# Row maxima of an attention kernel: how they are transposed, copied into q's tile, and shared out between two stages

## The chip, the core and the metric

The kernel runs on one core of a Trainium2 chip. The metric is the device time of one execution in microseconds. The core has five engines that run on their own instruction streams and meet at semaphores: TensorE (PE in the profile; its weight loads are PEld), VectorE (DVE), ScalarE (ACT), GpSimd (POOL) and SyncE (SP), which here does nothing but issue DMA transfers.

## The reference, cut to what matters

Four layers over a sequence of 2048 rows of 512 numbers, all in float32: a Fourier mixing layer (A), attention (B), A again and B again, each behind a layer norm and with a residual sum.

```python
def _A_ref(x, dft_seq_re, dft_seq_im, dft_hid_re, dft_hid_im):
    a = jnp.einsum("bsd,ed->bse", x, dft_hid_re)
    b = jnp.einsum("bsd,ed->bse", x, dft_hid_im)
    return jnp.einsum("ts,bse->bte", dft_seq_re, a) - jnp.einsum("ts,bse->bte", dft_seq_im, b)

def _B_ref(x, wq, wk, wv, wo):          # 32 heads of 16, one head of keys and values for all
    ...
    scores = jnp.einsum("bhqd,bkd->bhqk", q, k) * (Dh ** -0.5)
    p = _softmax(scores, axis=-1)
    o = jnp.einsum("bhqk,bkd->bhqd", p, v)
    return (lambda x, *d: x.transpose(*d))(o, 0, 2, 1, 3).reshape(B, S, H * Dh) @ wo

x = A_x
x = x + _A_ref(_layernorm(x, axis=-1), ...)
x = x + _B_ref(_layernorm(x, axis=-1), ...)
x = x + _A_ref(_layernorm(x, axis=-1), ...)
x = x + _B_ref(_layernorm(x, axis=-1), ...)
```

## The kernel before, in words

The program handles one Fourier layer and the attention layer behind it as a pair (`make_layer`), twice. `phase_a` is the Fourier stage and `phase_b` the attention stage. The order on each engine is the order in which the Python program writes the instructions; nothing is reordered afterwards, so a step's place in the loops sets its place in the queue of its engine.

**Precision.** Most products are made of three matmuls (`mm3`, L87 to L89) of a rounded high part and a low remainder. ScalarE makes the high part, GpSimd or VectorE the low one (`split_sb`, `split_act`, `split_ps`).

**Fourier stage.** 128 steps: four column blocks (`tb`) of 512, two parts (`c`, real and imaginary), sixteen row tiles (`s`). A step has four products of three matmuls. After each of the first three blocks come four `y_tile` calls, which multiply by the hidden Fourier matrix, add the residual and take layer norm's statistics. The block's rows are then normalized (`ln_apply`, L182), transposed, and multiplied to keys, values and queries while the next block's steps run (`prep_tasks`). Queries are stored to DRAM (`qd`) and loaded again by tile (`qT_load`, L356).

**Early maxima.** Softmax needs each row's maximum ahead of the exponentials. A unit of maxima is one tile of 128 queries against one block of 512 keys: 32 matmuls with a VectorE maximum each (`max_one`, L334 and L335). The list `EARLY` names the units that are done in the Fourier stage already: tile, key block, the buffer for q, the step at which q is loaded, and the first and last place between which the 32 pieces are spread. Places count 40 to a block: 32 steps, and 8 for the four `y_tile` calls, one place being twelve matmuls. Before, the list has 16 units. The others are done in the attention stage (`max_half`, L347 and L348). A maximum uses one of three PSUM banks named `y`.

**Attention stage.** 16 tiles of 32 steps. Each step has four score matmuls (`score`, L698, two to one exponential of ScalarE, L701), three maxima for a later tile, and the eight matmuls of p times v of the step before last (`pv`, L712). Score and maximum matmuls use half the rows of the array, and the order alternates the halves.

**The maxima's rows.** The negated maxima of a tile are made part of the score product: q's tile has two spare rows in each half (rows 48, 49 and 112, 113) that hold the maximum's high and low part, against ones in the key tile. At step 27 `max_neg` reduces the next tile's partial maxima to `ms`; at step 29 `max_rows` transposes `ms` on TensorE into a `y` bank, ScalarE copies the result to `mt`, and four DMAs from SyncE's queue copy 16 of its rows each into one spare row of q's tile (L376 to L383). The first score of the next tile is at step 0, three steps later. The same is done for the second half of tile 0 and of tile 15, at steps 11 and 13, for step 16, and once at the end of the Fourier stage, where two of the four DMAs go on ScalarE's queue.

**Output projection.** At step 12 `o_proj` makes twelve matmuls for the tile before; after every six of them it also does two maxima, and adds them to the allowance (`owed`) of maxima per step. VectorE then adds the residual (L777).

Of the kernel before, what the change touches and what calls it, by code (L numbers as in the profile page):

```python
# [8 lines left out]
F32 = mybir.dt.float32  # L9
F32R = mybir.dt.float32r  # L10
I32 = mybir.dt.int32
AF = mybir.ActivationFunctionType
ALU = mybir.AluOpType
# [4 lines left out]
P = 128  # L18
# [4 lines left out]
NT = S // P  # L23
# [9 lines left out]


EARLY = [
# [5 lines left out]
]  # L41
KEPT = [e for e in EARLY if e[0]]
QSLOT = (8, 0, 1, "h", "l", 8, 0, 1, "h", "l", 8, 0, 1, 8, 0, 1)
# [4 lines left out]
def fnet_mqa_kernel(ctx: ExitStack, tc: tile.TileContext, x_in, ct, dt_, wq, wkv, wo, out):  # L48
    nc = tc.nc
    ctx.enter_context(tc.manual_schedule())  # L50
    sb = ctx.enter_context(tc.tile_pool(name="sb", bufs=1, reuse_waits="tile"))
# [3 lines left out]
    def f(ap):  # L55
        return ap.bitcast(F32)

    def slot(k, dtype=F32):
        return sb.tile([P, S], dtype, name=f"slot{k}")

    def half(k, dtype=F32):
        return sb.tile([P, D], dtype, name=f"row{k}")

    def bank(tag):
        return ps.tile([P, 512], F32, name=tag, bufs={"y": 3, "z": 1}[tag])
# [25 lines left out]
    ident = sb.tile([P, P], F32, name="ident")  # L91
# [18 lines left out]
    mv = sb.tile([P, NT, 2], F32, name="mv")  # L110
    rs = sb.tile([P, NT], F32, name="rs")
# [41 lines left out]
    def ln_rstd(t0, n, table=True, between=lambda: None):  # L153
        v = sb.tile([P, 4], F32, name="lnv", bufs=2)[:, :n]
        w = sb.tile([P, 4], F32, name="lnw", bufs=2)[:, :n]
        r = rs[:, t0:t0 + n]
        nc.vector.tensor_scalar(v, mv[:, t0:t0 + n, 1], EPS, None, op0=ALU.add)
        if table:
            nc.scalar.activation(w, v, AF.Sqrt)
            between()  # L160
            nc.vector.reciprocal(r, w)
            between()
            rounds = 1
        else:
            nc.vector.tensor_scalar(w.bitcast(I32), v.bitcast(I32), 1, None, op0=ALU.logical_shift_right)
            nc.vector.tensor_scalar(r.bitcast(I32), w.bitcast(I32), -1, 0x5F3759DF, op0=ALU.mult, op1=ALU.add)
            rounds = 3
        e = nc.vector if table else nc.gpsimd
        for _ in range(rounds):
            if n == 1 and table:  # L170
                e.scalar_tensor_tensor(w, r, v, r, op0=ALU.mult, op1=ALU.mult)
            else:
                e.tensor_mul(w, r, r)
                e.tensor_mul(w, w, v)
            between()
            e.tensor_scalar(w, w, -0.5, 1.5, op0=ALU.mult, op1=ALU.add)
            between()
            e.tensor_mul(r, r, w)
            between()

    def ln_apply(dst, x, t, eng=None):
        (eng or nc.vector).tensor_scalar(dst, x, mv[:, t, 0:1], rs[:, t:t + 1], op0=ALU.subtract, op1=ALU.mult)  # L182

    class Layer:
        pass
# [1 line left out]
    def make_layer(L, src, mid, dst, last):  # L187
        o = Layer()
        raws = {}
        hls = {}  # L190
        st = {}
# [41 lines left out]
        def wq_load(g):  # L233
            st["wq", g] = half(g)
            nc.sync.dma_start(st["wq", g], wq[:, g, :])

        def wq_split(g):
            st["wqh", g] = hl_tiles()
            split_sb(st["wq", g], *st["wqh", g], nc.gpsimd)
# [6 lines left out]
        def tr_tile(t, x, xth, xtl, raw=None):  # L246
            pt = bank("z")
            for k in range(NK):
                nc.tensor.transpose(pt[:, k * P:(k + 1) * P], x[:, k * P:(k + 1) * P], ident)
            v = [ap.rearrange("p (a b) -> p a b", a=NK) for ap in (pt, raw or pt)]  # L250
            if raw:
                split_act(v[0], xth, xtl, v[1])
            else:
                split_ps(v[0], xth, xtl)

        def kv(t0, n, xth, xtl, vt=None):
            pk = bank("y")[:, :n * P]
            for k in range(NK):
                mm3(pk, wkvh[:, k, :], wkvl[:, k, :], xth[:, k, :n * P], xtl[:, k, :n * P], k == 0, k == NK - 1)
            cs = slice(t0 * P, (t0 + n) * P)  # L260
            if vt is None:
                vt = half(7)[:64, :n * P]
            nc.scalar.copy(vt[32:64], pk[32:64])
            for g in range(2):
                gs = slice(64 * g, 64 * g + 64)
                nc.scalar.activation(kz[g][gs, cs], pk[gs], AF.Identity, scale=kmask[gs], bias=kone[gs])
            for g in range(2):
                gs = slice(64 * g + 32, 64 * g + 48)
                nc.vector.tensor_sub(kz[g][gs, cs], pk[gs], f(kz[g][gs, cs]))
            return vt  # L270

        def v_tr(t0, n, vt):
            pv_ = bank("z")[:, :n * 32].rearrange("p (t d) -> p t d", t=n)
            for j in range(n):
                nc.tensor.transpose(pv_[:, j, :], vt[32:64, j * P:(j + 1) * P], ident[32:64, 32:64])
            nc.scalar.copy(v1[:, t0:t0 + n, :DH], pv_[:, :, DH:])
# [95 lines left out]

        def max_rows(i, p0=0, n=NPAIR, queue=None):
            queue = queue or nc.sync
            pt = bank("y")[:4 * n, :P]
            nc.tensor.transpose(pt, st["ms"].rearrange("p a b c -> p (a b c)"), ident)  # L376
            mt = sb.tile([64, P], F32R, name="mt")[:4 * n, :]
            nc.scalar.copy(mt, pt)  # L378
            for g in range(2):
                for r in range(2):  # L380
                    row = 64 * g + M0 + r
                    q = queue if r else nc.sync
                    q.dma_start(f(o.qT[i][row:row + 1, p0:p0 + n, :]), f(mt[n * (2 * g + r):n * (2 * g + r + 1), :]))  # L383

        def y_tile(tb, tt, zh, zl, x1, between={}):
            t = 4 * tb + tt
# [82 lines left out]
        def prep_tasks(tb, x1):  # L469
            base = 32 * (tb + 1)  # L470
            ts = {}

            def alloc():
                ln_rstd(4 * tb, 4)
                st["xt"] = [slot(2 + j, F32R).rearrange("p (k t) -> p k t", k=NK) for j in range(2)]

            def tr(tt):
                xth, xtl = st["xt"]
                cs = slice(tt * P, (tt + 1) * P)
                tr_tile(4 * tb + tt, x1[tt], xth[:, :, cs], xtl[:, :, cs], half(6 + tt % 2))  # L480

            def do_kv():
                st["vt"] = kv(4 * tb, 4, *st["xt"])

            ts[0] = [alloc, lambda: ln_apply(x1[0], x1[0], 4 * tb, nc.gpsimd)]
            for j in range(1, 4):
                ts[j] = [lambda j=j: ln_apply(x1[j], x1[j], 4 * tb + j, nc.gpsimd), lambda j=j: tr(j - 1)]
            ts[4] = [lambda: tr(3)]
            ts[4] += [lambda: [wq_load(g) for g in range(4)]]
            ts[5] = [do_kv]  # L490
            ts[6] = [lambda: wq_split(0), lambda: v_tr(4 * tb, 4, st["vt"])]
            for g in range(4):
                ts[7 + g] = [lambda g=g: q_mm(tb, g, *st["xt"])]
                if g:
                    ts[7 + g].append(lambda g=g: q_store(tb, g - 1))
                if g < 3:
                    ts[7 + g].append(lambda g=g: wq_split(g + 1))
            ts[11] = [lambda: q_store(tb, 3)]
            return {base + k: v for k, v in ts.items()}

        def phase_a(extra):
# [155 lines left out]
            for k in range(12):  # L657
                more_max()
                if k == 2:
# [3 lines left out]
        units = [(0, pr, g, 3) for pr in range(HALF, NPAIR) for g in range(2)]  # L663
        units += [(i, pr, g, kb) for i in range(1, NT) for pr in range(NPAIR) for kb in range(4) for g in range(2)
                  if (i, kb) not in early]
        o.done = o.extra = 0

        def more_max():
            if o.done < len(units) and units[o.done][0] in o.loaded | {0}:
                max_half(*units[o.done])  # L670
                o.done += 1

        def owed(n):
            return min(3 * (n + 1) + 12 + o.extra, len(units)) - o.done

        def done_with(i, pr):
            return all(u[:2] > (i, pr) for u in units[o.done:])
# [83 lines left out]
        def o_mm(k):  # L761
            if k == 0:
                bt["po"] = bank("y")
            ks = slice(k * P, (k + 1) * P)
            mm3(bt["po"], bt["oh"][:, ks], bt["ol"][:, ks], woh[:, k, :], wol[:, k, :], k == 0, k == NK - 1)

        def o_proj(i):
            for k in range(NK):
                o_mm(k)
                if k % 2 and i < NT - 1:  # L770
                    for _ in range(2):
                        more_max()
                        o.extra += 1
            o_add(i)

        def o_add(i):
# [170 lines left out]
```

## Time and profile before

| | |
|---|---|
| median of 3 runs | 3785.59 us (3784.23 to 3785.99) |
| the profiled execution | 3786.89 us |
| its span, first to last instruction | 3784.9 us |
| mean granted TensorE clock | 0.993 |
| first Fourier stage and start | 0 to 711 us |
| first attention stage | 711 to about 1890 us |
| second Fourier stage | to about 2592 us |
| second attention stage | to the end |
| busy: PE, DVE, ACT, POOL | 97%, 74%, 63%, 20% |

In the rows of the profile a line number is that of the kernel before. A group's row gives line, engine, operation, what is written and read, the count, the busy time with the mean of one in ns, and the idle time ahead of it with what ended it. A timeline's row gives start, busy time, engine, line, operation and how many instructions were merged. Engine names that end in q (SPq, ACTq) are the queue that issues DMAs: its bar is the time that the issue occupies the queue, not the transfer. Since matmuls overlap, their starts tell the pace and not their durations.

### The profile page before, as it was taken

The numbers are of one execution on the slowest core, as the hardware profiler recorded it, in microseconds if no ns is written. First come the engines' busy times: TensorE is split into PE (matmuls) and PEld (weight loads), VectorE is DVE, ScalarE is ACT, GpSimd is POOL, SyncE is SP. The second block draws the span as 40 slices with busy tenths as digits, with TensorE's granted clock in tenths as the row PEclk, the third lists the DMA queues.
The fourth block names the chain that finished last, engine by engine and source line by source line (L and its number), as shares of the span: only waits on it lengthen the run. The fifth ranks groups of instructions, "written<-read, shape, count | busy, mean of one in ns | idle before, by whom it ended". The sixth has DMA issues, their size and how long they took to land.

```text
span 3784.9 us, 56745 instructions
## 1 busy us (share of the span) xinstructions
PE 3675.7 (97%) x21826; PEld 1983.5 (52%) x21826; DVE 2814.5 (74%) x4759; ACT 2394.7 (63%) x2925; POOL 763.9 (20%) x914
## 2 busy tenths in 40 slices
PE   8989999999999999999999999999999999999999
PEld 6777778633333333333377777785333333333433
DVE  5165977688888888888411769777888888888882
ACT  3212211588888888888933221216888888888888
POOL 5634342201010000100155343421000000000000
PEclk9999999999999999999999999999999999999999
DMA  5543332311111100110133342413111111001100
GB/s 177 123 137 101 100 96 87 97 35 33 46 35 32 47 23 21 32 49 21 41 128 103 112 125 76 121 61 98 33 49 32 35 33 46 24 21 48 34 23 25
DMA packets 204703, 242.50 MB, mean 64 GB/s; under 512 B 36880, under 2 KB 160784, under 8 KB 197264
## 3 DMA queue, kind: packets, MB, share of 16 engines
q1 hardware_dynamic: 199504, 222.08, 19.3%
q0 software_dynamic: 4864, 16.78, 1.7%
q8 instruction: 171, 2.80, 0.3%
q14 instruction: 100, 0.82, 0.1%
q10 hardware_dynamic: 64, 0.02, 0.0%
HBM read 174.58 MB, written 63.17 MB: 63 GB/s over the span
## 4 chain that ended last, share of the span: by engine, by line
PE 80%; DVE 6%; ACT 3%; issue 3%; POOL 2%; DMA 1%; SPq 0%; POOLq 0%; ACTq 0%; DVEq 0%
PE z L712 24%; PE x L698 17%; PE y L347 10%; PE y L334 6%; PE x L87 5%; PE x L89 5%; PE x L88 5%; DVE mxp L348 4%; PE y L87 3%; PE y L89 2%; PE y L88 2%; ACT slot L701 1%; POOL row L182 1%; POOL cl L79 1%; POOL slot L84 1%
## 5 line engine op out<-in xcount | busy, mean ns | idle before, releaser
L701 ACT ACTIVATE slot<-x 128x1024 f32<-128x1024 f32 x1990 | 1943.8, 1027 | 323.8 <-PE x L698 271.1
L348 DVE TENSOR_REDUCE mxp<-y 128x1 f32<-128x512 f32 x3040 | 1907.3, 683 | 281.0 <-PE y L347 229.3
L712 PE MATMUL z<-slot,v 128*32 128x512 f32 x8192 | 1096.3, 605 | 1.9 <-ACT row L715 1.9
L698 PE MATMUL x<-slot,kz 64*128 64x512 f32 x2956 | 904.1, 446 | 5.5 <-DMA slot<-mt 5.4
L698 PEld LDWEIGHTS x<-slot,kz 64*128 64x128 f32 x2956 | 375.0, 185 | 733.3 <-ACT slot L701 603.0
L347 PE MATMUL y<-kz,slot 64*128 64x512 f32 x2272 | 751.6, 437 | 5.4 <-ACT mt L378 0.7
L335 DVE TENSOR_REDUCE mxe<-y 128x1 f32<-128x512 f32 x832 | 525.0, 683 | 124.4 <-PE y L334 123.7
L87 PE MATMUL x<-ch,xnh 128*128 128x512 f32 (+1 forms) x1152 | 432.3, 375 | 14.7 <-ACT xnh L449 10.3
L89 PE MATMUL x<-ch,xnl 128*128 128x512 f32 (+1 forms) x1152 | 429.6, 373 | 1.6 <-POOL xnl L450 1.2
L88 PE MATMUL x<-cl,xnh 128*128 128x512 f32 (+1 forms) x1152 | 428.2, 372 | 0.4 <-POOL cl L79 0.4
L334 PE MATMUL y<-kz,slot 128*128 128x512 f32 (+1 forms) x1088 | 380.9, 399 | 44.9 <-DMA slot<-qd 16.1
L347 PEld LDWEIGHTS y<-kz,slot 64*128 64x128 f32 x2272 | 360.2, 185 | 102.9 <-DVE mxp L348 31.9
L78 ACT CAST ch<-craw 128x512 fp32r<-128x512 f32 x256 | 156.4, 619 | 385.0 <-PE x L89 362.7
L79 POOL TENSOR_TENSOR cl<-craw,ch 128x512 fp32r<-128x512 f32 x236 | 307.9, 1311 | 352.9 <-ACT ch L78 285.7
L712 PEld LDWEIGHTS z<-slot,v 128*32 128x32 f32 x8192 | 163.6, 108 | 280.8 <-issue 252.7
L752 POOL TENSOR_TENSOR row<-row,row 128x256 f32<-128x256 f32 x63 | 46.2, 734 | 1190.3 <-DMA row<-rd 620.7
L334 PEld LDWEIGHTS y<-kz,slot 128*128 128x128 f32 x1088 | 203.8, 190 | 107.9 <-DVE mxe L335 27.6
L87 PEld LDWEIGHTS x<-ch,xnh 128*128 128x128 f32 x1152 | 219.3, 190 | 55.0 <-ACT xnh L449 10.8
L89 PEld LDWEIGHTS x<-ch,xnl 128*128 128x128 f32 x1152 | 218.8, 190 | 44.8 <-POOL xnl L450 4.9
L88 PEld LDWEIGHTS x<-cl,xnh 128*128 128x128 f32 x1152 | 219.1, 190 | 43.4 <-POOL cl L79 0.7
L335 DVE TENSOR_REDUCE mxp<-y 128x1 f32<-128x512 f32 (+1 forms) x256 | 145.9, 617 | 128.7 <-PE y L334 127.9
L87 PE MATMUL y<-slot,slot 128*128 128x512 f32 x384 | 157.7, 411 | 5.8 <-DVE mxe L335 1.7
(144 smaller groups left out, 2825.7 us busy)
## 6 DMA issues: line engine op xcount, KB each, us to landing
craw<-ct_in SPq DMA_DIRECT2D x112, 512.0 KB
slot<-qd SPq DMA_DIRECT2D x44, 1024.0 KB
qd<-row SPq DMA_DIRECT2D x144, 128.0 KB
od<-row SPq DMA_DIRECT2D x252, 64.0 KB
row<-x_in SPq DMA_DIRECT2D x32, 256.0 KB
mid<-row POOLq DMA_DIRECT2D x32, 256.0 KB, 2.3
craw<-ct_in SPq DMA_DIRECT2D x32, 256.0 KB
row<-mid SPq DMA_DIRECT2D x32, 256.0 KB
```

Source lines behind the costliest of these rows:

```text
L78: nc.scalar.copy(hi, raw)
L79: (eng or nc.vector).tensor_sub(lo, raw, f(hi))
L87: nc.tensor.matmul(ps_, ah, bh, start=start, stop=False)
L88: nc.tensor.matmul(ps_, ah, bl, start=False, stop=False)
L89: nc.tensor.matmul(ps_, al, bh, start=False, stop=stop)
L334: nc.tensor.matmul(pm, o.qT[i][:, pr, :], kz[g][:, c0:c0 + n], start=True, stop=True)
L335: nc.vector.reduce_max(to, pm, axis=AX.X)
L347: nc.tensor.matmul(pm, o.qT[i][gs, pr, :], kz[g][gs, kb * 512:kb * 512 + 512], start=True, stop=True)
L348: nc.vector.reduce_max(partial(i)[:, pr, g, kb:kb + 1], pm, axis=AX.X)
L698: nc.tensor.matmul(st["e"][:, g, :], kz[g][64 * g:64 * g + KR, c * P:(c + 1) * P], o.qT[i][64 * g:64 * g + KR, cp:cp + 4, :], start=True, ...
L701: nc.scalar.activation(ptiles[i, s_][:, 2 * w:2 * w + 2, :], st.pop("e"), AF.Exp, scale=DH ** -0.5)
L712: nc.tensor.matmul(a[32 * j:32 * j + 32, :], v1[:, c, :], pt[:, j, :], start=c == 0, stop=c == NT - 1)
```

## The change

Three edits and a re-made list:

- `EARLY` has 18 units and not 16, the first one starts at place 56 and not 53.5, and most of the later ones span about 4 places. `o_proj` does no maxima any more, and the allowance per step loses the term that counted them.
- `max_rows` transposes `ms` on VectorE in blocks of 32x32 straight into `mt`, without TensorE, a PSUM bank or ScalarE. Since blocks are transposed each in its place, a row of 128 queries lies in four pieces of 32 columns on four groups of partitions, so each row is copied by four DMAs: sixteen for four rows.
- `ln_apply` in `prep_tasks` goes from GpSimd to VectorE.

```diff
 EARLY = [
-    (0, 0, 2, 44, 53.5, 59.5), (1, 0, 3, 44, 59.5, 65), (2, 0, 2, 52, 65, 70.5), (3, 0, 8, 50, 70.5, 86),
-    (0, 1, 0, 66, 86, 90.5), (1, 1, 1, 66, 90.5, 94.5), (3, 1, 8, None, 94.5, 99.5),
-    (4, 0, 2, 78, 99.5, 104.5), (4, 1, 2, None, 104.5, 109.5), (5, 0, 8, 84, 109.5, 116),
-    (5, 1, 8, None, 116, 123), (6, 0, 0, 97, 123, 128), (6, 1, 0, None, 128, 133),
-    (7, 0, 2, 107, 133, 137.5), (7, 1, 2, None, 137.5, 142), (0, 2, 8, 101, 142, 147),
+    (0, 0, 2, 44, 56, 61.5), (1, 0, 3, 44, 61.5, 66.5), (2, 0, 2, 54, 66.5, 70.9), (3, 0, 8, 50, 70.9, 87),
+    (0, 1, 0, 66, 87, 91), (1, 1, 1, 66, 91, 94.7), (3, 1, 8, None, 94.7, 98.7),
+    (4, 0, 2, 78, 98.7, 102.7), (4, 1, 2, None, 102.7, 106.7), (5, 0, 3, 78, 106.7, 110.7),
+    (6, 0, 8, 84, 110.7, 116), (6, 1, 8, None, 116, 122.5), (7, 0, 0, 97, 122.5, 126.5),
+    (7, 1, 0, None, 126.5, 130.5), (5, 1, 1, 97, 130.5, 134.6), (2, 1, 2, 108, 134.6, 138.6),
+    (2, 2, 2, None, 138.6, 142.6), (0, 2, 8, 101, 142.6, 148.5),
 ]
...
-    def ln_apply(dst, x, t, eng=None):
-        (eng or nc.vector).tensor_scalar(dst, x, mv[:, t, 0:1], rs[:, t:t + 1], op0=ALU.subtract, op1=ALU.mult)
+    def ln_apply(dst, x, t):
+        nc.vector.tensor_scalar(dst, x, mv[:, t, 0:1], rs[:, t:t + 1], op0=ALU.subtract, op1=ALU.mult)
...
         def max_rows(i, p0=0, n=NPAIR, queue=None):
             queue = queue or nc.sync
-            pt = bank("y")[:4 * n, :P]
-            nc.tensor.transpose(pt, st["ms"].rearrange("p a b c -> p (a b c)"), ident)
-            mt = sb.tile([64, P], F32R, name="mt")[:4 * n, :]
-            nc.scalar.copy(mt, pt)
+            mt = sb.tile([P, 64], F32, name="mt")[:, :4 * n]
+            nc.vector.transpose(mt, st["ms"].rearrange("p a b c -> p (a b c)"))
             for g in range(2):
                 for r in range(2):
                     row = 64 * g + M0 + r
+                    b, c = divmod(n * (2 * g + r), 32)
                     q = queue if r else nc.sync
-                    q.dma_start(f(o.qT[i][row:row + 1, p0:p0 + n, :]), f(mt[n * (2 * g + r):n * (2 * g + r + 1), :]))
+                    for a in range(4):
+                        q.dma_start(f(o.qT[i][row:row + 1, p0:p0 + n, 32 * a:32 * a + 32]),
+                                    mt[32 * a + c:32 * a + c + n, 32 * b:32 * b + 32])
...
-            ts[0] = [alloc, lambda: ln_apply(x1[0], x1[0], 4 * tb, nc.gpsimd)]
+            ts[0] = [alloc, lambda: ln_apply(x1[0], x1[0], 4 * tb)]
             for j in range(1, 4):
-                ts[j] = [lambda j=j: ln_apply(x1[j], x1[j], 4 * tb + j, nc.gpsimd), lambda j=j: tr(j - 1)]
+                ts[j] = [lambda j=j: ln_apply(x1[j], x1[j], 4 * tb + j), lambda j=j: tr(j - 1)]
...
-            return min(3 * (n + 1) + 12 + o.extra, len(units)) - o.done
+            return min(3 * (n + 1) + 12, len(units)) - o.done
...
             for k in range(NK):
                 o_mm(k)
-                if k % 2 and i < NT - 1:
-                    for _ in range(2):
-                        more_max()
-                        o.extra += 1
             o_add(i)
```

More of the change, by code (lines that the diff above doesn't have):

```diff
@@ L665, in make_layer @@
                   if (i, kb) not in early]
-        o.done = o.extra = 0
+        o.done = 0
         def more_max():
```

## The prediction

> **What bounds the kernel now.** I read the page's engine totals and groups first, then the timelines of TensorE, VectorE and SyncE's queue around one tile of the attention stage, then the chain that ended last at tile boundaries, then windows with the granted clock around the known TensorE gaps.
>
> ```profile
> PE 3675.7 (97%) x21826; PEld 1983.5 (52%) x21826; DVE 2814.5 (74%) x4759; ACT 2394.7 (63%) x2925; POOL 763.9 (20%) x914
> L348 DVE TENSOR_REDUCE mxp<-y 128x1 f32<-128x512 f32 x3040 | 1907.3, 683 | 281.0 <-PE y L347 229.3
> 1554.37 1.07 PE L712 MATMUL z<-slot,v 128*32 128x512 f32 x8
> 1556.49 1.06 PE L712 MATMUL z<-slot,v 128*32 128x512 f32 x8
> 1558.80 0.50 PE L87 MATMUL y<-slot,slot 128*128 128x512 f32 x1
> 1560.39 0.50 PE L347 MATMUL y<-kz,slot 64*128 64x512 f32 x2
> 1562.42 0.51 PE L347 MATMUL y<-kz,slot 64*128 64x512 f32 x2
> 1562.86 1.07 PE L712 MATMUL z<-slot,v 128*32 128x512 f32 x8
> 1565.55 1.07 PE L712 MATMUL z<-slot,v 128*32 128x512 f32 x8
> 1564.16 0.68 DVE L777 TENSOR_TENSOR row<-y,row 128x512 f32<-128x512 f32 x1
> ```
>
> The reader is to see that TensorE sets the pace: an attention step runs from one group of eight L712 matmuls to the next, 1556.49 - 1554.37 = 2.12 us, and VectorE's three maxima fit in. The step that holds the output projection takes 1562.86 - 1556.49 = 6.37 us, and the one after it 2.69 us.
>
> At a tile boundary the maxima's rows have to be in q's tile before the next tile's first score:
>
> ```profile
> 1597.93 3.67 DVE L348 TENSOR_REDUCE mxp<-y 128x1 f32<-128x512 f32 x6
> 1601.96 0.26 ACT L378 CAST mt<-y 64x128 fp32r<-64x128 f32 x1
> 1602.25 2.46 SPq L383 DMA_DIRECT2D slot<-mt  x4
> 1605.06 1.06 PE L712 MATMUL z<-slot,v 128*32 128x512 f32 x8
> 1606.11 0.47 PE L698 MATMUL x<-slot,kz 64*128 64x512 f32 x1
> 750.37 1.76 DMA slot<-mt
> 752.27 0.47 PE x L698
> L383 SPq DMA_DIRECT2D slot<-mt x108: 562/590/1553, 709.8 to 3741.2; - x108
> L204 SPq DMA_DIRECT2D craw<-ct_in x112: 323/328/711, 1.7 to 2424.5; - x112
> L725 SPq DMA_DIRECT2D od<-row x252: 303/436/1775, 756.1 to 3747.4; - x126
> ```
>
> Four row copies occupy SyncE's queue for 2.46 us; one is 0.590 us and they start (2.46 - 0.59)/3 = 0.623 us apart. They begin at 1602.25, so the queue is done at 1604.71, and the first score starts at 1606.11, 1.40 us later. Where the copy is on the chain, it takes 1.76 us from the end of its issue. So there is no slack at this place: every microsecond that the last copy is later is a microsecond that TensorE stands still.
>
> **The change, part by part.**
>
> *Row copies: four become sixteen.* Each `max_rows` in the attention stage now issues four 32-column pieces for each of four rows, all on SyncE. The 8 KB and 4 KB copies of today share one row, 562 to 590 ns, so I see no dependence on size, and I take 0.623 us a copy: 12 x 0.623 = 7.48 us later. Ends: 0.36 us (the 0.328 of L204 plus the same gap of 0.033 between two) gives 16 x 0.36 - 2.46 = 3.3 us; 0.69 (the 0.646 of the same copy on ScalarE's queue, shown below) gives 12 x 0.69 = 8.3 us.
>
> *Transpose on VectorE instead of TensorE and ScalarE.* The old path ends 1602.25 - 1601.60 = 0.65 us after the maxima of that step (1597.93 + 3.67). The new one is an operation of 128x64 on VectorE behind the same maxima. The trace has none; nearest rows:
>
> ```profile
> L363 DVE TENSOR_REDUCE nm<-mxp 128x32 f32<-128x128 f32 (+2 forms) x36 | 9.4, 260 | 0.1
> L370 DVE TENSOR_TENSOR ms<-nm,ms 128x32 fp32r<-128x32 f32 (+1 forms) x36 | 6.8, 189 | 1.2
> L369 DVE CAST ms<-nm 128x32 fp32r<-128x32 f32 (+1 forms) x36 | 12.6, 349 | 1.2
> L376 PE MATMUL y<-ident,ms 128*64 128x128 f32 (+1 forms) x36 | 10.6, 295 | 1.1 <-DVE mxp L348 1.1
> ```
>
> I take 0.26 (it reads about as much as L363; ends 0.19 and 0.35), so the first copy can go 0.35 us sooner. VectorE's 36 x 0.26 = 9 us lie in the 0.24 us that it idles in each step. What goes on TensorE (36 x 0.295) and ScalarE is worth nothing, since both then stand at the copies. Net delay: 7.48 - 0.35 = 7.1 us a boundary (3.0 to 8.0). The score that comes first belongs to the upper half (the unit that is due is of half 0, so the order starts with half 1), whose rows are copied last, so TensorE does nothing meanwhile. Behind the sixteen in SyncE's queue stands the store of the attention output (L725), whose source is made one step after the stalled score, so it waits for nothing new.
>
> *The clock after a gap.* TensorE has two gaps of this length today, both waits for q:
>
> ```profile
> PE y L334 <- DMA slot<-qd: 16.1, 2, 8.9
> 195.00:196.50 1.50, 0.00 (x0) 0.00 (x0) 0.00 (x0) 0.00 (x0) 1.50 (x3) 1.00 0.74 262
> 198.00:199.50 1.50, 0.00 (x0) 0.00 (x0) 0.00 (x0) 0.00 (x0) 0.00 (x0) 0.89 0.72 112
> 202.50:204.00 1.50, 0.30 (x1) 0.30 (x2) 0.00 (x0) 0.00 (x0) 0.00 (x0) 0.50 0.99 377
> 208.50:210.00 1.50, 1.50 (x6) 1.16 (x5) 0.72 (x2) 0.00 (x0) 0.00 (x0) 0.70 0.42 96
> 2079.00:2080.50 1.50, 0.52 (x3) 0.08 (x1) 0.00 (x0) 0.00 (x0) 0.62 (x1) 1.00 0.79 292
> 2082.00:2083.50 1.50, 0.00 (x0) 0.00 (x0) 0.00 (x0) 0.00 (x0) 0.00 (x0) 0.94 0.99 377
> 2089.50:2091.00 1.50, 1.50 (x7) 1.20 (x6) 0.75 (x2) 0.52 (x1) 0.91 (x1) 0.79 0.03 14
> ```
>
> The column after the five engines is the granted clock. It falls to 0.50 about 4 us into the gap and returns some 6 and 3.5 us after work resumes (at 203.2 and 2086.8), so the slow stretch costs about 3.0 and 1.6 us. A 7.1 us gap is long enough: 2.3 us a boundary (0 to 3.0).
>
> *Count.* Per layer 15 boundaries to the next tile and one for tile 0's second half: 32 x (7.1 + 2.3) = 301 us. Tile 15's second half has no maxima left, so its transpose is not held to the step but only to the projection's sum; its copies can start about 2.6 us sooner than now and the delay is near 5: 2 x (5.1 + 2.3) = 15. At the start of the attention stage eight copies go on SyncE and eight on ScalarE:
>
> ```profile
> L383 ACTq DMA_DIRECT2D slot<-mt x4: 627/646/1314, 709.8 to 2591.7; - x4
> 714.87 0.43 PE x L698
> ```
>
> 709.5 + 8 x 0.69 + 1.77 = 716.8 against the score at 714.87: 2 us, twice, 4. Sum of the copies: +320 us.
>
> *No maxima in the output projection.* Fourteen projections per layer carry four (the fifteenth comes when all are done). Without them the step is 2.12 + 0.19 (switch) + 12 x 0.233 = 5.1 instead of 6.37, and the sum (L777) no longer waits behind two maxima, so the following step is 2.12, not 2.69: 1.25 + 0.57 = 1.8 us, 28 times, -50 us (ends -35 and -62; the latter if all four maxima, 4 x 0.6 on VectorE, had been paid). The allowance of maxima per step is lowered with them, so no step gets more.
>
> *Two more early units, the list shifted.* 64 more maxima per layer in the Fourier stage. The spacings there:
>
> ```profile
> 453.25 3.08 DVE L335 TENSOR_REDUCE mxe<-y 128x1 f32<-128x512 f32 x5 [0.19 <-PE y L334]
> 456.50 1.89 DVE L335 TENSOR_REDUCE mxe<-y 128x1 f32<-128x512 f32 x3 [0.17 <-PE y L334]
> 459.07 0.39 PE L89 MATMUL x<-ch,xnl 128*128 128x512 f32 x1
> 459.30 0.39 PE L334 MATMUL y<-kz,slot 128*128 128x512 f32 x1
> L249 PE MATMUL z<-ident,row 128*128 128x128 f32 x128 | 20.1, 280 | 10.6 <-POOL row L182 10.4
> L182 POOL TENSOR_SCALAR row<-row,mv,rs 128x512 f32<-128x512 f32 x24 | 49.7, 2071 | 10.6 <-DVE rs L178 10.6
> ```
>
> TensorE: 128 x 0.23 = +29 us. Eleven units are now four steps long: VectorE needs 32 x 0.595 = 19.0 us for one ((3.08 - 1.89)/2), TensorE (48 + 32) x 0.23 = 18.4, so it becomes the bound there by about 0.7 a unit: 22 x 0.7 = +16 (0 to 40, if its other work there shows too). The first unit starts 2.5 steps later, 2.5 x 12 x 0.23 = 6.9 us, which covers most of the 8.9 and 7.3 us waits for q and the slow clock after them: -(6.9 + 3.0) - (6.9 + 1.6) = -18.
>
> *Layer norm's apply on VectorE.* 24 x 2.07 us leave GpSimd, where the split pieces stand behind them; TensorE waits 10.4 us for them in all. I take -6 (0 to -10); on VectorE 24 pieces of about 0.55 fall where the list of maxima is thin. Fourier stages together: 29 + 16 - 18 - 6 = +21.
>
> **Sum.** 320 - 50 + 21 = +291 us on the profiled execution's 3786.9, which stands 1.3 above the median of the runs: 4076 against 3785.6.
>
> **Rivals.**
> (a) *A copy is cheap when it is small.* The pieces move 128 B runs instead of 512 B. If the queue's time a copy falls so far that sixteen end no later than four do now, no boundary moves, and what is left is -50 + 21: 3757. It decides at (2.46 + 0.35 + 29/34)/16 = 0.23 us a copy: below that the change is faster. For it speaks that no copy of this exact form is in the trace; against it that the fastest of 252 stores of L725 took 0.303 and that half the bytes cost the same 0.59 today. [...]
> (b) *A copy takes the short form's 0.36 us.* Then the gap is 3.3 - 0.35 = 3.0 us, too short for the clock to fall: 34 x 3.0 = 102, with -50 + 21: 3859. For it: many SyncE issues take 0.33. Against: those are plain whole-partition blocks, and this copy gathers 16 partitions into one, as today's does.
> (c) *All as forecast, but the clock stays up*, because the transposes, or work that I count as waiting, fill the gap: 4076 - 34 x 2.3 = 3998. It lies within my own range.
>
> **How the numbers follow.** My forecast with (c) has 0.80, (b) 0.09, (a) 0.11. The likeliest case's own range is 3960 to 4140: without the clock's loss and with cheap dense units at one end, with 0.69 us a copy and most of the upper bounds at the other. The range given reaches down to (b), 3850 to 4140. About 0.2% can be told from no change here (7.6 us): (b) and the forecast are slower, 0.89; (a) splits into 0.08 faster and 0.03 the same, if its dense units cost their upper bound.
>
> **What would show it.** SyncE's queue should show sixteen copies of near 0.6 us at each boundary, some 10 us long; the first score of each tile should wait 7 us for a copy into q's tile, and those waits sum to over 200 us; in the slices the granted clock should fall below 1 once per tile, every 80 us or so; the output projection's step should shrink to 5.1 us and the early maxima run back to back on VectorE. The wait for q at 195 us should nearly vanish. The prediction is wrong if a copy's bar is near 0.2 us, if the scores do not wait for the copies, or if the dense units cost several times 16 us.

## The result and the profile after

| | before | changed kernel |
|---|---|---|
| median | 3784.91 us (3781.85 to 3785.99) | 4088.22 us (4088.04 to 4090.14) |
| profiled span | 3784.9 us | 4088.4 us |
| mean granted TensorE clock | 0.993 | 0.950 |

The ratio is 1.0804 (95% interval 1.0785 to 1.0823): 303 us slower. The forecast was 4076 us, in a range of 3850 to 4140.

The totals, the granted clock in 40 slices, the group of the score matmuls and the waits of TensorE, all of the changed kernel (its lines stand two after those of before from the middle of the program on):

```profile
PE 3734.2 (91%) x21790; PEld 2010.0 (49%) x21790; DVE 2824.0 (69%) x4819; ACT 2392.0 (59%) x2893; POOL 713.9 (17%) x894
PEclk9999999899999999999899999998999999989998
L700 PE MATMUL x<-slot,kz 64*128 64x512 f32 x2948 | 925.8, 458 | 207.9 <-DMA slot<-mt 206.7
PE x L700 <- DMA slot<-mt: 206.7, 30, 9.1
PE x L700 <- DMA xnh<-mt: 30.8, 4, 8.1
PE x L700 <- DMA xnl<-mt: 30.0, 4, 7.9
PE y L348 <- DMA slot<-qd: 10.2, 2, 5.3
PE y L335 <- DMA slot<-qd: 2.6, 1, 2.6
PE z L250 <- DVE row L183: 1.6, 4, 0.5
```

The busy times are nearly those of before; TensorE's share fell from 97% to 91% because the span grew around it. The score matmuls now wait 206.7 + 30.8 + 30.0 = 267.5 us for the row copies from `mt`; before, that wait was 5.8 us in all. The row below these three is a wait that I had not forecast, of a maximum's matmul in the attention stage for q (10.2 us). The two waits of before for the first q tile (16.1 us) have shrunk to 2.6, the row after it.

One tile boundary of the changed kernel, in order of time, and the granted clock (the column after the five engines) around it:

```profile
1617.55 3.67 DVE L349 TENSOR_REDUCE mxp<-y 128x1 f32<-128x512 f32 x6
1621.14 0.23 DVE L377 STREAM_TRANSPOSE mt<-ms 128x64 f32<-128x64 f32 x1
1621.44 10.52 SPq L384 DMA_DIRECT2D slot<-mt  x16
1624.39 1.07 PE L714 MATMUL z<-slot,v 128*32 128x512 f32 x8
1633.60 0.76 PE L700 MATMUL x<-slot,kz 64*128 64x512 f32 x1 [8.14 <-DMA slot<-mt]
1635.60 1.94 PE L714 MATMUL z<-slot,v 128*32 128x512 f32 x8
1638.38 1.06 PE L714 MATMUL z<-slot,v 128*32 128x512 f32 x8
1626.50:1628.00 1.50, 0.00 (x0) 0.00 (x0) 0.00 (x0) 0.00 (x0) 0.00 (x0) 0.77 0.03 3
1635.50:1637.00 1.50, 1.50 (x9) 0.20 (x8) 0.82 (x2) 1.35 (x2) 0.00 (x0) 0.50 0.00 0
1638.50:1640.00 1.50, 1.39 (x10) 0.22 (x7) 0.25 (x1) 1.50 (x2) 0.00 (x0) 1.00 0.42 87
```

The reader is to see the transpose on VectorE end 0.07 us ahead of the first copy (1621.44 - 1621.14 - 0.23), sixteen copies fill SyncE's queue for 10.52 us, and TensorE stand for 8.14 us. This is one of the longer queues: the median of the changed kernel is 10.05 us. About 2 us into that gap the clock falls to half, and it is still there when work resumes: the eight L714 matmuls take 1.94 us and not 1.06. From 1624.39 to 1635.60 is 11.2 us for a step of 2.2 us in the kernel before, and the next one is longer too.

**Where the 303 us went.** Both profiles give the start of every step's L712 (L714) matmuls, so the difference can be added up by the place of the step in its tile. From the profiled executions:

| place | forecast | measured, both layers |
|---|---|---|
| 30 boundaries to the next tile (steps 0 and 1) | +282 | +143.7 + 146.2 = +290 |
| second halves of tiles 0 and 15 (steps 16, 17) | +19 + 15 | +15.6 + 18.1 = +34 |
| projection (steps 12, 13) | -50 | -23.9 - 24.0 = -48 |
| Fourier stages, and the start of the attention stages | +21 + 4 | +10.0 + 11.4 = +21 |
| tile 11, steps 3 to 5 | none | +8.8 + 8.9 = +18 |
| steps 27 to 31 | none | -4.4 - 6.7 = -11 |

The rest is under 1 us.

### The profile page after: what moved, and what is told of

It reads as the page before. It is cut to its first block, busy times and chain, and to the rows that moved or that the text cites. A ratio compares the mean times of both kernels' runs of the same rounds, so it can differ in the third digit from the quotient of the medians.

```text
span 4088.4 us, 57271 instructions
## 1 busy us (share of the span) xinstructions
PE 3734.2 (91%) x21790; PEld 2010.0 (49%) x21790; DVE 2824.0 (69%) x4819; ACT 2392.0 (59%) x2893; POOL 713.9 (17%) x894
## 5 line engine op out<-in xcount | busy, mean ns | idle before, releaser
L349 DVE TENSOR_REDUCE mxp<-y 128x1 f32<-128x512 f32 x2912 | 1825.3, 683 | 565.1 <-PE y L348 488.0
L714 PE MATMUL z<-slot,v 128*32 128x512 f32 x8192 | 1129.9, 623 | 0.0
L700 PE MATMUL x<-slot,kz 64*128 64x512 f32 x2948 | 925.8, 458 | 207.9 <-DMA slot<-mt 206.7
L700 PEld LDWEIGHTS x<-slot,kz 64*128 64x128 f32 x2948 | 401.2, 193 | 965.1 <-ACT slot L703 586.7
L348 PE MATMUL y<-kz,slot 64*128 64x512 f32 x2144 | 734.1, 447 | 15.3 <-DMA slot<-qd 10.2
L336 DVE TENSOR_REDUCE mxe<-y 128x1 f32<-128x512 f32 x960 | 591.4, 680 | 87.3 <-PE y L335 86.4
L335 PE MATMUL y<-kz,slot 128*128 128x512 f32 (+1 forms) x1216 | 416.8, 405 | 29.4 <-DVE mxe L336 16.7
L714 PEld LDWEIGHTS z<-slot,v 128*32 128x32 f32 x8192 | 165.7, 109 | 300.1 <-issue 285.1
L335 PEld LDWEIGHTS y<-kz,slot 128*128 128x128 f32 x1216 | 229.0, 189 | 134.4 <-DVE mxe L336 76.0
L700 PE MATMUL x<-xnh,kz 64*128 64x512 f32 x512 | 160.7, 454 | 30.8 <-DMA xnh<-mt 30.8
L700 PE MATMUL x<-xnl,kz 64*128 64x512 f32 x512 | 160.7, 453 | 30.0 <-DMA xnl<-mt 30.0
```

The lines of the kernel that those rows point to most:

```text
L335: nc.tensor.matmul(pm, o.qT[i][:, pr, :], kz[g][:, c0:c0 + n], start=True, stop=True)
L336: nc.vector.reduce_max(to, pm, axis=AX.X)
L348: nc.tensor.matmul(pm, o.qT[i][gs, pr, :], kz[g][gs, kb * 512:kb * 512 + 512], start=True, stop=True)
L349: nc.vector.reduce_max(partial(i)[:, pr, g, kb:kb + 1], pm, axis=AX.X)
L700: nc.tensor.matmul(st["e"][:, g, :], kz[g][64 * g:64 * g + KR, c * P:(c + 1) * P], o.qT[i][64 * g:64 * g + KR, cp:cp + 4, :], start=True, ...
L714: nc.tensor.matmul(a[32 * j:32 * j + 32, :], v1[:, c, :], pt[:, j, :], start=c == 0, stop=c == NT - 1)
```

## The experiments

All times are medians; a ratio is to the kernel before, run on the same chip beside it, with its 95% interval.

**Undoing the row copies alone.** The changed kernel with the old `max_rows`; to find room, `mt` lies in one of the `craw` buffers.

```diff
-            mt = sb.tile([P, 64], F32, name="mt")[:, :4 * n]
-            nc.vector.transpose(mt, st["ms"].rearrange("p a b c -> p (a b c)"))
+            pt = bank("y")[:4 * n, :P]
+            nc.tensor.transpose(pt, st["ms"].rearrange("p a b c -> p (a b c)"), ident)
+            mt = raw_tile()[:4 * n, 0, :P].bitcast(F32R)
+            nc.scalar.copy(mt, pt)
...             (four copies, as before)
```

> The changed kernel with max_rows as it was before (transpose on TensorE, copy on ScalarE, four row copies); the early list, the projection without maxima and layer norm on VectorE stay. Theory (sixteen issues stand on SyncE's queue in front of each tile's first score): the boundaries lose their 324 us, and the old transpose gives back some 11 us in steps 28 to 30, so about 3773 us, 12 under the kernel before, made of +21 (Fourier stages), -48 (projection), +18 (a late load of q's tile 13 at tile 11, which stays). Rival 1 (the projection's gain is only possible because the stalls let VectorE catch up): step 12 goes back towards 6.3 us and the time is about 3820. Rival 2 (the early list or layer norm on VectorE carries a good part of the loss): over 3850.

Measured: 3772.49 us, ratio 0.9965 (0.9952 to 0.9978). By steps, the boundaries are back within 0.3 us of before in sum, the projection keeps its -23.5 and -23.4 us, and tile 11 keeps its late load, +9.6 and +9.0 in steps 3 to 5. So the other edits gain 13 us together, and rivals 1 and 2 fall.

**Doing the row copies alone.** The kernel before with the new `max_rows`.

```diff
-            nc.tensor.transpose(pt, st["ms"].rearrange("p a b c -> p (a b c)"), ident)
-            nc.scalar.copy(mt, pt)
+            nc.vector.transpose(mt, st["ms"].rearrange("p a b c -> p (a b c)"))
...             (sixteen copies, as in the change)
```

> The kernel before with the new max_rows alone (transpose on VectorE, sixteen row copies). Theory: 30 boundaries at 9.7 us, the four half tiles 34 us, the start of the attention stages 4, less 11 in the last steps: 3785 + 317 = about 4100 us. Rival 1 (loss only together with the denser list or the changed order of maxima): under 3900. Rival 2 (the stall gives VectorE and ScalarE time that the projection's maxima then use): some 20 us less, about 4080.

Measured: 4098.11 us, ratio 1.0824 (1.0806 to 1.0842). The loss needs nothing but this edit; the waits of TensorE for the copies are those of the changed kernel (204.6 + 30.8 + 30.1 us).

**Half as many copies, the low part left out.** The changed kernel copies only the high part's rows, so its exponentials miss the low part of the maxima.

```diff
-                for r in range(2):
+                for r in range(1):
```

> The changed kernel that copies only the high part of the maxima, 8 copies a tile instead of 16; the low part's rows stay zero. Theory (wait = issue time beyond the lead, and a slow clock only after a gap of about 4 us): the wait falls from 8.1 to 8.1 - 8 x 0.657 = 2.9 us, the granted clock stays at 1.00, each boundary gives back 5.3 + 1.6, so 4088 - 34 x 6.9 = about 3855. Rival 1 (the slow clock costs nothing): only 34 x 5.3 come back, about 3908. Rival 2 (the wait is one of landing, not of issue: small copies land late): the wait hardly changes, over 4000.

Measured: 3886.45 us, ratio 1.0264 (1.0248 to 1.0279), 31 us over the theory and 22 under the first rival. The waits behaved: 86.1 us over 36 score matmuls, 2.4 us each, so 181 of the 202 us that came back are waits. The clock did not: its mean is 0.974 and not 0.99. That a gap must last about 4 us for the clock to fall was wrong.

**The same copies, sent earlier (e4).** The changed kernel with the lead raised, nothing else.

```diff
-AHEAD = 5
+AHEAD = 9
```

> The changed kernel with the maxima reduced and sent at step 23 and not at step 27 (AHEAD 9 for 5), all sixteen copies kept. Theory: seven steps are 15 us, the copies need 0.2 + 10.5 + 1.9 = 12.6, so no first score waits and the clock stays up: 4088 - 324 = about 3764, with the 10.5 us on SyncE's queue still in the trace. Rival 1 (the copies cost by themselves, by their transfers or their semaphores): over 3900. Rival 2 (on the queue they now collide with the output's loads at step 23): the projection waits, 3800 to 3850.

Measured: 3760.61 us, ratio 0.9933 (0.9918 to 0.9948). SyncE's queue of this kernel at a boundary, and TensorE's wait for the copies:

```profile
1506.83 10.27 SPq L384 DMA_DIRECT2D slot<-mt  x16
PE x L700 <- DMA slot<-mt: 8.3, 4, 3.5
```

All sixteen copies are there and take as long as ever; only their start is four steps earlier, and the waits go from 267.5 to 8.3 us. So the price was neither the transfers nor the transpose, but issue time that stood past the lead.

**All data in half as many copies.** The two rows of a half lie on adjacent partitions in the source and in the destination, so one copy can carry both: 8 copies of twice the size, nothing left out, at the old lead.

```diff
-                for r in range(2):
-                    row = 64 * g + M0 + r
-                    b, c = divmod(n * (2 * g + r), 32)
+                row = 64 * g + M0
+                b, c = divmod(n * 2 * g, 32)
...
-                        q.dma_start(f(o.qT[i][row:row + 1, p0:p0 + n, 32 * a:32 * a + 32]),
-                                    mt[32 * a + c:32 * a + c + n, 32 * b:32 * b + 32])
+                    q.dma_start(f(o.qT[i][row:row + 2, p0:p0 + n, 32 * a:32 * a + 32]),
+                                mt[32 * a + c:32 * a + c + 2 * n, 32 * b:32 * b + 32])
```

> The changed kernel with the high and the low row of a half in one copy: 8 copies of twice the size a tile, all data copied, sent at step 27 and 29 as in the changed kernel. Theory (the price is the number of issues, not bytes or pieces): the same as with 8 copies of the high part alone, 3886 us. Rival 1 (the price goes with the bytes or the 128 B pieces, which are those of the changed kernel): near 4088. Rival 2 (a copy with twice the partitions takes longer to issue): between, 3930 to 4000.

Measured: 3874.32 us, ratio 1.0233 (1.0216 to 1.0250). A copy of twice the data, in the same 128 B pieces, takes the queue nearly as long (a median of 611 ns, against 588 in the changed kernel), and the wait is near that of eight copies: 79.8 us at the thirty boundaries against 73.4:

```profile
L383 SPq DMA_DIRECT2D slot<-mt x216: 598/611/807, 714.3 to 3832.0; - x108
PE x L699 <- DMA slot<-mt: 65.9, 26, 3.0
PE x L699 <- DMA xnl<-mt: 10.2, 4, 2.6
PE x L699 <- DMA xnh<-mt: 10.2, 4, 2.6
```

So here the number of issues sets the price, and bytes or pieces hardly count. This run also prices the clock by itself. In eleven of its thirty boundaries to the next tile the clock stays up, and these cost 2.6 us on average against the kernel before; in the other nineteen, with nearly the same wait (2.7 us for 2.6), it falls and they cost 4.4. Two boundaries of this kernel, each in a stretch with the wait and one behind it:

```profile
1019.00:1022.00 3.00, 0.95 (x7) 0.73 (x7) 0.41 (x1) 0.21 (x2) 0.00 (x0) 1.00 0.03 4
1022.00:1027.00 5.00, 5.00 (x37) 1.81 (x38) 4.45 (x8) 4.96 (x6) 0.00 (x0) 1.00 0.26 55
1710.70:1713.70 3.00, 0.89 (x4) 0.90 (x6) 0.06 (x1) 0.00 (x0) 0.00 (x0) 0.81 0.03 5
1713.70:1718.70 5.00, 5.00 (x23) 1.74 (x21) 2.99 (x5) 2.95 (x4) 0.00 (x0) 0.50 0.07 16
```

TensorE is as idle in the one as in the other, 2.0 to 2.1 of 3 us. In the next 5 us it starts 37 matmuls at full clock, 23 at half.

What tells them apart can be read from the traces. All 19 changes of the granted clock in the trace of the kernel before lie on one grid, at multiples of 3.4133 us from each other to within 0.001 us, and so do the 89 in that of the changed kernel. Here are the same two boundaries of this run, cut into cells of that length (1709.12 - 1016.21 is 203 of them):

```profile
1016.21:1019.63 3.41, 2.31 (x19) 0.82 (x15) 2.34 (x4) 2.70 (x3) 0.00 (x0) 1.00 0.04 6
1019.63:1023.04 3.41, 1.99 (x15) 0.89 (x15) 1.45 (x3) 1.16 (x2) 0.00 (x0) 1.00 0.04 7
1709.12:1712.53 3.41, 0.65 (x8) 0.00 (x0) 0.90 (x2) 1.22 (x2) 0.00 (x0) 1.00 0.04 8
1712.53:1715.95 3.41, 3.14 (x15) 1.47 (x15) 1.89 (x3) 1.82 (x2) 0.00 (x0) 0.50 0.00 0
```

The first wait is shared by two cells of the grid, and TensorE is busy for more than half of each (2.31 and 1.99 us of 3.41); the second leaves one cell with 0.65 us of work, and the next cell runs at half clock. In the sixty boundaries of the two runs with eight copies at the old lead, all 46 that lose the clock have a cell with TensorE busy for at most 0.47 of it, and all 14 that keep it have none under 0.50. Outside these boundaries the share does not part them: a cell with 1.65 us of work is followed by a slow one in the changed kernel (at 890.03 us) and by a fast one in the kernel before (at 2479.27), and at the start of the attention stages of both the clock falls behind cells with 2.25 to 2.69 us of work.

**The late q tile (e5).** On top of the earlier send: q is loaded at step 0 and not at step 2 of its tile, and its maxima are held back until step 3 is over.

```diff
-                if s_ == 2:
-                    for j in range(2, NT):
-                        if i == max(0, j - 4 if j < 13 else j - 2):
-                            qT_load(j)
+                for j in range(2, NT):
+                    if i == max(0, j - 4 if j < 13 else j - 2):
+                        if s_ == (0 if i else 2):
+                            qT_load(j)
+                            if i:
+                                o.loaded.discard(j)
+                        if i and s_ == 3:
+                            o.loaded.add(j)
```

> e4 (maxima sent at step 23) with q's tiles loaded at step 0 of their tile and not at step 2, and their maxima held back until step 3 is over. Theory (at tile 11 the stream of maxima has reached tile 13, whose q is loaded at step 2 into the buffer that tile 10 has just left, so TensorE waits 5 us and the clock falls): the wait of 5.2 us per layer and its slow clock go, some 21 us in both layers less about 4 for catching up at four maxima a step: 3761 - 17 = about 3744. Rival (held-back maxima make VectorE the bound and give it all back): 3758 to 3762.

Measured: 3746.26 us, ratio 0.9900 (0.9887 to 0.9914), 14 us under e4. The wait of the maxima for q is gone from the list of waits; tile 11 still costs 4.6 us a layer over the kernel before, the four maxima a step by which it catches up.

**Layer norm's apply back on GpSimd**, on e5 (one argument in two places: `ln_apply(x1[j], x1[j], 4 * tb + j, nc.gpsimd)`).

> The same as e5 with layer norm's apply on GpSimd again, as in the kernel before. Theory (the move to VectorE was worth the waits of TensorE for it, 10.4 us in the kernel before, of which some are taken by the next piece in line): 6 us more than e5. Rival 1 (VectorE is so full with 18 early units that the move costs what it brings): the same within 3 us. Rival 2: GpSimd is better now, e6 is faster.

Measured: 3758.95 us, ratio 0.9934 (0.9922 to 0.9947): 12.7 us more than e5, twice the theory. TensorE's wait, 1.6 us in e5, is back in its old size:

```profile
PE z L250 <- POOL row L183: 10.5, 12, 2.2
```

These are 8.9 us of the 12.7; what the rest is, is not shown.

**The first early units at their old places**, on e5.

```diff
-    (0, 0, 2, 44, 56, 61.5), (1, 0, 3, 44, 61.5, 66.5), (2, 0, 2, 54, 66.5, 70.9), (3, 0, 8, 50, 70.9, 87),
+    (0, 0, 2, 44, 53.5, 59.5), (1, 0, 3, 44, 59.5, 65), (2, 0, 2, 52, 65, 70.5), (3, 0, 8, 50, 70.5, 87),
```

> The same as e5 with the first three early units at their places of before (53.5, 59.5 and 65, and q's third load at 52). Theory (the shift by 2.5 places was worth 18 us: it covers the two waits for the first q tile, 8.9 and 7.3 us, and the slow clock behind them): 18 us more than e5. Rival (the list is bound by VectorE, so an earlier start gives back what the wait takes): within 5 us of e5.

Measured: 3765.05 us, ratio 0.9946 (0.9933 to 0.9960): 18.8 us more, and the wait for the first q tile is back:

```profile
PE y L335 <- DMA slot<-qd: 17.6, 2, 10.4
```

**Pairs and the earlier send together.**

> The same as e5 with the high and the low row of a half in one copy: 8 copies of twice the size a tile, nothing left out. Theory: the queue is behind seven steps of cover in either case, so only the half tiles' waits (8.3 us in e4) and the start of the attention stages (some 5 us) can go: 5 to 10 us less than e5. Rival (nothing waits for the queue any more): the same within 3 us.

Measured: 3738.83 us, ratio 0.9881 (0.9867 to 0.9894), 7 us under e5, as far as the spread of their runs (3735 to 3744, 3745 to 3749) can tell them apart. The two profiled executions are too close (3742.3 and 3742.9 us of span) to show where the difference lies. It is the fastest kernel of this study, 45 us or 1.2% under the kernel before.

**The old transposes with the earlier send.** The old `max_rows` with the lead of 9 and q loaded early.

> The old max_rows (TensorE, ScalarE, four copies) with the new list, no maxima in the projection, the maxima sent at step 23 and q loaded at step 0. Theory (with the wait gone, the transpose on VectorE keeps the 9.6 us per layer that steps 27 to 31 show, since TensorE and a PSUM bank are spared): about 3744 + 19 = 3763, less a few us as the old copy's own waits go too, 3758. Rival (those steps gain only by where the maxima are reduced, at step 23): the same as e5 within 4 us.

Measured: 3743.41 us, ratio 0.9889 (0.9874 to 0.9904), a miss: I expected 3758, and the rival holds. Steps 27 to 31 gain 9.9 us a layer here too. Reducing the maxima at step 23 takes that work out of them and adds it at steps 22 to 26: 3.0 us a layer with the new transpose, 6.6 with the old. So with enough lead the transpose on VectorE is worth some 3.5 us a layer in these steps. In whole times it does not show. The second Fourier stage and the start behind it take 712.1 us with the old rows, 714.7 with sixteen copies and 711.1 with pairs; the first stage and its start take 723.4, 724.3 and 727.9, another order. What the longer queue costs there is therefore not shown, and no ranking of old rows against the other two holds beyond the spread.

## Why the prediction was right, step by step

*Row copies.* The mechanism is shown three ways: undone alone it gives the loss back, done alone it makes it, and with the same copies sent earlier it is gone. The term was +320 and measured 290 + 34 + 1 = 325 (the 1 is for the start of the attention stages, as the run with the row copies alone has it), but its two parts were off in opposite ways. The wait was larger: at the thirty boundaries to the next tile it grew from 3.9 to 230.4 us, 7.55 a boundary against 7.1. Sixteen copies hold the queue 10.23 us on average where four hold it 2.55, which is 7.68 longer and close to the 7.48 of the sum; but the first copy starts only 0.13 us earlier against the step that waits, not 0.35, since the steps of TensorE ahead of it got shorter as well. The clock was smaller: 290/30 = 9.7 us a boundary less 7.55 leaves 2.1, against 2.3. The shorter gaps of the pairs give 4.4 - 2.6 = 1.8.

*The clock's threshold.* "Long enough" was right for 7.1 us: the changed kernel's gaps of 7.2 to 8.6 us lost the clock at all thirty boundaries, 1.8 to 5.1 us after they began. The threshold of 4 us was wrong: with eight copies 46 of the sixty boundaries lost it, at waits of 2.4 us on average over e3's thirty and of 2.7 over e9's nineteen that lost it. In the two gaps that the 4 us were read from, the clock fell at 199.16 and 2083.32 us, 4.3 and 3.8 us after they began. Both are the end of the first cell of the grid that stood idle as a whole (0.00 us of work, behind cells with 2.51 and 3.03). Rival (b) rested on the 4 us; with a gap of 3.0 us its 3859 would have been too low, by an estimate of some 30 us, as the eight copies missed their theory by 31.

*The transpose.* It was costed at 0.26 us and takes 0.23; the copies begin 0.07 us behind it. That the work taken from TensorE and ScalarE was worth nothing was wrong by 11 us: steps 27 to 31 come ahead of the stall. They gain 4.3 and 6.3 us a layer with the new rows alone, and nothing (+0.3 and +0.2) where the old rows are put back.

*The projection.* -50 forecast, -48 measured. In the kernel before, its step and the next took 6.34 and 2.71 us in the middle of the tiles, now 5.26 and 2.12.

*The Fourier stages.* +21 came out as +20 (21 less 1.4 that the copies alone cost there), but by luck in part, with errors that cancel: layer norm's apply was worth 12.7 and not 6, the shift of the first units 18.8 for 18, so if the parts simply add, the two units with their dense places cost about 51, not 45. No run has them alone.

*What was left out.* The step "the allowance of maxima per step is lowered with them, so no step gets more" looked at how many maxima a step gets and not at which. With 64 fewer maxima in its way the stream reaches tile 13 at step 1 of tile 11 (at step 9 before), and the load of that tile's q is written at step 2 of tile 11, into the buffer that tile 10 has just left. The changed kernel there:

```profile
1642.57 0.38 SPq L357 DMA_DIRECT2D slot<-qd  x1
1647.56 0.80 PE L348 MATMUL y<-kz,slot 64*128 64x512 f32 x2 [5.33 <-DMA slot<-qd]
```

A wait of 5.3 us, a slow clock and maxima to catch up on cost 18 us in both layers. That the load would be met too early could be counted from the code beforehand. These +18 us and the -11 us of the steps ahead of the stall were both missing from the sum, and that they nearly cancel is luck: with the +18 alone the result would stand 23 us above the forecast and not 12.

*Rival (a)* is refuted: no copy was cheap for being small. The row that the prediction took to show one price for 8 KB and 4 KB gives the least and the median of both; by themselves the 4 KB copies of before took longer, 626 ns or more. On the chip the 128 B copies take a median of 588 ns where the 512 B ones took 590:

```profile
L384 SPq DMA_DIRECT2D slot<-mt x432: 515/588/1602, 716.8 to 4041.9; - x144
```

In the stall the DMA engines are nearly idle (busy share 0.03), and the split into sixteen finishes 7.5 us later: what is full is the queue that issues them, for 10.52 us at the boundary shown. The idle DMA engines agree that this time is not the data's; what the queue does in it no run here shows.

## What to carry to other kernels

A copy of this form, sixteen rows into one, costs its queue about 0.6 us with pieces of 512 B or of 128 B (medians of 590 and 588 ns; other forms in the same trace take 0.33), so an edit that spares three cheap instructions and splits four copies into sixteen has to be charged 12 x 0.6 us wherever something waits for the last of them. Before giving such a chain up, look at its lead: here one constant (nine steps for five) turned a loss of 8% into a gain of 0.7%, and with q loaded in time and paired copies 1.2%. When work is moved out of a stream that runs ahead, ask which load the stream will meet earlier.

## What the runs showed of the hardware that was not expected

Short gaps on TensorE halved its clock too, in the run with pairs at nineteen of thirty boundaries, at 2.7 us of wait on average, and these cost 1.8 us more than the eleven that kept it. At these boundaries it went with how the gap lay on the grid of 3.413 us. In the run with pairs nine boundaries in a row, some 75 us or 22 cells of the grid apart, kept the full clock, and the following six all lost it, with much the same wait. In the changed kernel the gaps of 7.2 to 8.6 us halved the clock at all thirty boundaries; in the run with pairs a boundary with TensorE idle for 2.1 us did so too.

The copies start 0.62 us apart in most rows of four and 0.63 in most rows of eight or sixteen of the changed kernel and the run with eight; some rows, as the one shown, have 0.66. Why was not tried.
